# The backward weave of a gated attention pair: when ridden rows, sweep chunks and weights are loaded

## The chip, the cores and the metric

One core of one Trainium2 chip runs the whole kernel as one launch. The metric is device microseconds of one execution, median of several runs. The profile is of one further execution. Engines are named as the profile names them: PE (TensorE matmuls) with PEld (its weight loads), DVE (VectorE), ACT (ScalarE), POOL (GpSimd), SP (SyncE, which here only issues DMAs). Each of SP and POOL works through its own list in order, and an entry that waits holds all entries behind it.

## The reference

A token-wise gate mixes two attention branches over 2048 tokens of width 576, and all gradients are wanted.

```python
def _fwd_reference(A_x, A_wq, ..., B_Wo, B_seg_len, gate_w):
    ...
        scores = jnp.einsum('bhqd,bkd->bhqk', q, k) * Dh ** (-0.5)   # branch A: 32 query heads of 18, one key/value head
        p = _softmax(scores, axis=-1)
    ...
        for s in range(n_seg):                                       # branch B: 64 segments of 32 tokens
            xs = x[:, s * seg_len:(s + 1) * seg_len, :].copy()
            h = jnp.concatenate([mem, xs], axis=1)                   # 8 memory rows ahead of 32 tokens
            ...
            o = jnp.einsum('bhte,hed->btd', o, Wo)
            mem = o[:, :M, :].copy()                                 # the recurrence
    ...
    g = _sigmoid((x * gate_w).sum(-1, keepdims=True))
    return g * a + (1 - g) * b

def reference(...):
    _out, _vjp = jax.vjp(_f, A_x, A_wq, A_wk, A_wv, A_wo, B_mem0, B_Wq, B_Wk, B_Wv, B_Wo, gate_w)
    _grads = _vjp(grad_out)
    return (_out, *_grads)
```

Branch B's recurrence makes its backward pass a chain of 64 segments, one after the other, from segment 63 down to 0. Branch A's backward pass has no such chain.

## The kernel before

The stages follow each other: projections, a forward weave, a token stage (`b_bulk`, which does what of branch B's backward pass needs no chain), the backward weave, a stage behind the chain (`b_post`), the weight gradients and branch A's end. The change lies in the backward weave and in the last part of the token stage. Lines are those of the kernel before.

**The weave.** `weave` (L274) lays two generators into one program order: the chain `b_chain_bwd` (L1001) and the sweep `a_pass2` (L1910), with a third generator `bwd_weights` (L649) that loads weights. One step, number i, runs the sweep to its next `yield`, lets the chain go on if i is in `prime`, and then lets the weights go on by one load. First `lead` = 12 such steps run, in which the chain is let on only in steps 2 and 5 (its memsets and first loads). From then on every chain place is followed by a step, until the chain is at its end; what is left of the sweep would run last. The order is written out by hand (`manual_schedule`): no scheduler moves an instruction.

**The sweep** has 1024 pairs of heads and 128-query blocks, one per step. Step n issues `b_S` (scores, PE) of pair n+1 into a single PSUM buffer, `b_dP` (PE) of pair n, the exponential `b_E` (ACT, L1951) of pair n+1, two products `b_dS` (DVE, L1974) and four `b_acc` matmuls of pair n-1. Its input comes in chunks: chunk c holds the queries of pairs 4c to 4c+3 in one of three buffers `b_QS` of 256 KB. In the token stage, eight groups before its loop ends, `sweep_first` (L1903) loads chunks 0 and 1. Each later chunk is loaded by SP in steps n with n % 4 = 2 (`load`, L1926, issue at L1932): chunk n/4+2, which waits until the last `b_acc` of chunk c-3, two steps earlier, is done, and is first read by the `b_S` that is issued in step n+5.

**The chain.** A segment has 16 places, each ended by a `yield`; this text counts them 1 to 16. Segment 63 has no places 1 to 3. In places 1 to 3 the gradient of the 8 memory rows (`dm`) is projected with `WoT`. Place 4 builds `r_dOT`, `r_prod` and the first `mem_grad`; its POOL work ends with four small DMAs to `dOm_dram`. Place 5 takes the softmax back (`r_dS`, `r_dSB`). Places 6 to 15 hold 48 units of `heads`, which multiply `dT` with the weights `WT`: value weights first (to place 9), then query weights (to place 12), then key weights (to place 15). Place 16 turns the sum into the next `dm`. The tile `dT` has three parts of 32 columns per head: 8 columns come from `mem_cols` (L1168), in place 5 (value), 8 (query) and 9 (key), and 24 are token rows that ride along so that 32 columns are full. These ridden rows are loaded by `load_dT` (L1040, a DMA that transposes, issue at L1043) for the next segment: value in place 11, query in place 14, key in place 16. That is done for segments 54 to 0. `load_a`, `load_b` and `load_c` bring the other inputs of the next segment, in places 6, 9 and 12. `kv_mm` and `kv_out`, in segments 59 to 16, compute key and value gradients of tokens beside the chain, with loads on SP (L1076 to L1083) and stores on POOL.

**The weights.** `WT` has 24 tiles of 576 KB (value 0 to 7, query 8 to 15, key 16 to 23). The token stage loads 0 to 11, as its ring of buffers comes free. `bwd_weights` loads the rest, one per step, and then `WoT`:

```python
        for j in range(12, 24):
            self.load_WT(j, pool)
            yield
        for kt in range(4):
            self.nc.sync.dma_start(self.WoT[0][:, kt, :], self.st_WoT[kt])
            yield
        self.nc.sync.dma_start(self.WoT[1][:], self.st_WoTt[:])
        yield
```

So 17 loads stand in steps 0 to 16: twelve of 576 KB, four of 1 MB, one of 512 KB. `WoT` is first read in place 1 of segment 62.

**The loads' limit.** The DMAs of SP take turns on eight semaphores, and so do those of POOL: a DMA is not issued before the one eight entries ahead of it in the same list has landed.

Of the kernel before, what the change touches and what calls it, by code (L numbers as in the profile page):

```python
# [12 lines left out]
BF16 = mybir.dt.bfloat16  # L13
# [3 lines left out]
P = 128  # L17
# [29 lines left out]
class Kern:  # L47
# [229 lines left out]
    def weave(self, chain, sweep, lead, prime=(), early=()):  # L277
        steps = itertools.count()
        early = iter(early)

        def step():
            i = next(steps)
            next(sweep, None)
            if i in prime:
                next(chain)
            next(early, None)

        for _ in range(lead):
            step()
        for _ in chain:  # L290
            step()
        for _ in sweep:
            pass
# [708 lines left out]
    def b_chain_bwd(self, wot, sp, kd, kvp, keep, psum):  # L1002
        nc = self.nc
# [12 lines left out]
        f = lambda ap: ap.rearrange("p c q -> p (c q)")  # L1016
# [18 lines left out]
        def load_c(s):  # L1035
            nc.sync.dma_start(mrow["dx"][0:32].rearrange("p u e -> p (u e)"),
                              self.dmx_dram[s * 8:s * 8 + 8].rearrange("m (c u) w e -> (m c) (u w e)", u=8))
            nc.sync.dma_start(mrow["q"][:].rearrange("p u e -> p (u e)"), self.row_dram["q"][s])

        def load_dT(s, wi):  # L1040
            if 0 <= s < NSEG - KR:
                t0 = T - RIDE * (NSEG - KR - s)
                nc.sync.dma_start_transpose(dT[:, wi], self.xtok[("dq", "dk", "dv")[wi]][t0:t0 + 32, :])  # L1043
# [14 lines left out]
        def x_rows(s, x, src):  # L1058
            xq = sp.tile([P, 2, 32], BF16, name=f"r_xq{x}", bufs=1)
            nc.vector.transpose(f(xq[:]), src)  # L1060
            nc.gpsimd.dma_start(self.pq_dram[s // 4].rearrange("c i q s h x k -> (c i q) s h x k")
                                [:, s % 4, :, x, 32 * (s % 4):32 * (s % 4) + 32], xq[:])
# [65 lines left out]
        for s in reversed(range(NSEG)):  # L1128
# [12 lines left out]
            for k, parts in enumerate((((0, (0, 1, 2)),), ((0, (3, 4)), (1, (0, 1))), ((1, (2, 3, 4)),))):  # L1141
                if s == NSEG - 1:
                    break
                for j, kts in parts:
                    self.proj_part(pj[j], d_, self.WoT, j, kts)
                    if kts[-1] == 4:
                        self.evac(dOm[:, 4 * j:4 * j + 4, :].rearrange("p u e -> p (u e)"), pj[j][:], use="s")
                if k == 1:
                    x_rows(s, 0, pT[:, 0, :])
                yield  # L1150
            src = self.mem_T(dOm, psum, "r_x", 1)
            dOT = sp.tile([P, 8, 4, 8], BF16, name="r_dOT", bufs=1)
# [47 lines left out]
            def heads(n):  # L1200
                for _ in range(n):
                    wi, u, cp = next(units)
                    for g in range(4):
                        h, hf = 8 * (2 * cp + g // 2) + u, g % 2
                        self.mm(ph[32 * g:32 * g + 32, :], lhsT=dT[:, wi, h, :],
                                rhs=self.WTs(wi, h, 2 * GD * hf, 2 * GD),
                                start=(wi == 2 and u + cp == 0), stop=(wi == 1 and u + cp == 8), tp=(0, 32 * g))
# [26 lines left out]
            yield  # L1234
            kv_out(n0 + 1)
            heads(7)
            load_dT(s - 1, 2)
            if s:
                pad_in("p", nxt["pT"][:, 1, :])
            yield  # L1240
            heads(7)
            if s:
                load_c(s - 1)
            yield
# [4 lines left out]
            yield  # L1249
            kv_out(n0 + 2)  # L1250
            heads(7)
            load_dT(s - 1, 0)
            if n0 == -4:
                kv_load(0)
            yield
# [20 lines left out]
            dn = dm[1 - s % 2]  # L1276
            nc.scalar.copy(dn[:, :, 0:8], pm[:])
            nc.gpsimd.dma_start(self.dxr_dram[s], hs[0:64].rearrange("p k c -> p (k c)"))
            load_dT(s - 1, 1)
            yield  # L1280
        pt = psum.tile([P, 8, P], BF16, name="r_x", bufs=1)
        for kt in range(NKT):
# [618 lines left out]
        dq_.dma_start(self.qs_blk(b, 1).rearrange("a p c -> p a c"), qt[:].rearrange("p a t x -> p a (t x)"))  # L1901

    def sweep_first(self):  # L1903
        self.QS = [self.wr.tile([P, 2, 512], BF16, name=f"b_QS{c}", bufs=1) for c in range(2)]
        self.KVb = [self.wr.tile([P, 512], BF16, name="b_KV0", bufs=1)]
        self.nc.sync.dma_start(self.KVb[0][:], self.kv_dram[:, 0:512])
        for c in range(2):
            self.nc.sync.dma_start(self.QS[c][:], self.qs_dram[0, c])

    def a_pass2(self, keep, sp, kvp, psum):  # L1910
        nc = self.nc
        T, NTT = self.T, self.NTT
        KV = {}

        def load_KV(kb):
            if kb < 4:
                KV[kb] = self.KVb[kb % 2]
                if kb:
                    nc.sync.dma_start(KV[kb][:], self.kv_dram[:, kb * 512:kb * 512 + 512])

        self.QS.append(sp.tile([P, 2, 512], BF16, name="b_QS2", bufs=1))
        self.KVb.append(keep.tile([P, 512], BF16, name="b_KV1", bufs=1))
        load_KV(0)
        Q, S, E_, D_ = {}, {}, {}, {}
        NC = 4 * NPR * NTT // 4

        def load(c):
            if c < NC:
                p, q4 = (c // 4) % NPR, c % 4
                QS = self.QS[c % 3]  # L1930
                if c > 1:
                    nc.sync.dma_start(QS[:], self.qs_dram[p, q4])  # L1932
                Q[c] = (QS[:, 0, :], QS[:, 1, :].rearrange("p (a b) -> p a b", b=P))

        def pair(n):
            return n // (NPR * NTT), n // 4, n % 4

        def mm_u(dst, n, base):
            kb, c, j = pair(n)
            for i in range(2):  # L1940
                r = slice(base + 32 * i, base + 32 * i + 32)
                self.mm(dst[i], lhsT=Q[c][0][r, j * P:j * P + P], rhs=KV[kb][r, :],
                        tp=(base + 32 * i, 0))

        def mm_S(n):
            S[n] = psum.tile([P, 2, 512], F32, name="b_S", bufs=1)
            mm_u([S[n][:, i, :] for i in range(2)], n, 0)

        def ex(n):
            E_[n] = sp.tile([P, 2, 512], BF16, name="b_E", bufs=3)  # L1950
            nc.scalar.activation(E_[n][:], S.pop(n)[:], ACT.Exp, scale=SCALEA)  # L1951

        load(0)
        load(1)
        mm_S(0)
        ex(0)
        acc = None
        NS = NPR * NTT
        NP_ = 4 * NS
        for n in range(NP_ + 1):  # L1960
            if n < NP_:
                if n % 4 == 2:
                    load(n // 4 + 2)
                if n % NS == NS // 2:
                    load_KV(n // NS + 1)
                if n + 1 < NP_:
                    mm_S(n + 1)
                dP = [psum.tile([P, 512], F32, name="b_dP", bufs=3) for _ in range(2)]
                mm_u([t[:] for t in dP], n, 64)
                if n + 1 < NP_:  # L1970
                    ex(n + 1)
                D_[n] = sp.tile([P, 2, 512], BF16, name="b_dS", bufs=2)
                for i in range(2):
                    nc.vector.tensor_tensor(out=D_[n][:, i, :], in0=dP[i][:], in1=E_[n][:, i, :], op=ALU.mult)  # L1974
            if n > 0:
                o = n - 1
                if o % NS == 0:
                    acc = psum.tile([P, 512], F32, name="b_acc", bufs=1)
                SD = Q[o // 4][1]
                src = (D_.pop(o), E_.pop(o))  # L1980
                for i4 in range(4):
                    self.mm(acc[32 * i4:32 * i4 + 32, :], lhsT=SD[:, o % 4, 32 * i4:32 * i4 + 32],
                            rhs=src[i4 // 2][:, i4 % 2, :],
                            start=(o % NS == 0), stop=(o % NS == NS - 1), tp=(0, 32 * i4))
                if o % NS == NS - 1:
                    dkv = kvp.tile([P, 4, P], BF16, name="r_kvo", bufs=2)
                    nc.scalar.copy(dkv[:].rearrange("p i e -> p (i e)"), acc[:])
                    k0 = (o // NS) * 512
                    nc.gpsimd.dma_start(self.dkv_dram[:, k0:k0 + 512], dkv[:].rearrange("p i e -> p (i e)"))
            yield  # L1990
# [103 lines left out]
def build_full(tc, A_x, A_wq, A_wk, A_wv, A_wo, B_mem0, B_Wq, B_Wk, B_Wv, B_Wo, gate_w, grad_out, outs_raw,  # L2094
               dbg=None):
    nc = tc.nc
# [4 lines left out]
    k = Kern(tc, T, A_x, A_wq, A_wk, A_wv, A_wo, B_mem0, B_Wq, B_Wk, B_Wv, B_Wo, gate_w, grad_out, outs=outs)  # L2101
# [3 lines left out]
    with SB("const") as cpool, tc.tile_pool(name="dram", bufs=1, space=bass.MemoryType.DRAM) as dram:  # L2105
# [18 lines left out]
        with ExitStack() as man:  # L2124
# [39 lines left out]
            twp = tw.enter_context(SB("tw"))  # L2164
            with SB("a3s", RIGHT) as a3s, SB("a3k", RIGHT) as a3k, SB("rw") as rw, SB("rs") as rs, \
                    SB("rd") as rd, SB("rk") as rk, SB("rv") as rv, PS("rp") as rp, PS("a3p") as a3p:
                k.weave(k.b_chain_bwd(rw, rs, rd, rv, rk, rp), k.a_pass2(a3k, a3s, rv, a3p), 12, (2, 5),
                        k.bwd_weights(twp))
            wHs = ExitStack()
            wH = wHs.enter_context(SB("wH", RIGHT))  # L2170
# [84 lines left out]
```

## Time and profile before

| | us |
|---|---|
| median of 3 runs | 5364.2 (5357.48 to 5371.53) |
| the profiled execution | 5351.38 |
| its span, from first to last instruction | 5349.7 |
| backward weave, first `b_S` to the last `dm` (2670.55 to 4326.3) | 1655.8 |
| of it up to place 1 of segment 62 (2732.82) | 62.3 |

The page gives busy time of each engine, the span in 40 slices, DMA queues, the chain of work that ended last, and the costliest groups of instructions. Other views list instructions in order of time, the waits of one engine with what ended them, and busy time in chosen stretches. "idle before" in brackets is the time that the engine stood still ahead of an instruction, with what ended it. A matmul's duration is partly modelled, so the gaps say more than the busy shares.

### The profile page before, as it was taken

How to read it: one execution, taken by the hardware profiler on the slowest of the kernel's cores; microseconds unless marked ns; L12 is line 12 of the kernel's file. 1: busy time of each engine (PE TensorE's matmuls, PEld its weight loads, DVE VectorE, ACT ScalarE, POOL GpSimd, SP SyncE). 2: the span in 40 equal slices, each digit the busy share in tenths (PEclk: the TensorE clock that was granted, in tenths of full speed). 3: DMA queues.
4: the chain of work that ended last, by engine and by line, in shares of the span. 5: the costliest groups of instructions: out<-in, count | busy, mean ns of one | idle time of the engine just before them, and what ended most of it. 6: DMA issues, size and time to landing. Idle time of an engine off the chain costs nothing.

```text
span 5349.7 us, 218056 instructions
## 1 busy us (share of the span) xinstructions
PE 5023.2 (94%) x93298; PEld 2941.2 (55%) x93476; DVE 3619.4 (68%) x7146; ACT 3323.5 (62%) x4816; POOL 2421.1 (45%) x4634
## 2 busy tenths in 40 slices
PE   7999999999999998988879999999999999999999
PEld 5434555555555555777735555555554467764444
DVE  5337888888888887777778888888888831111112
ACT  4327888888888886666668888888887732111101
POOL 4004555555555554444436666666654321222223
PEclk9999999999999999999989999999999999999999
DMA  6655655665665445878866889888876679976653
GB/s 217 227 182 131 146 140 143 140 144 144 140 143 131 119 107 181 247 235 241 242 202 170 193 196 199 199 197 200 196 172 140 148 165 224 265 229 210 195 175 114
DMA packets 1115775, 961.45 MB, mean 180 GB/s; under 512 B 690738, under 2 KB 942139, under 8 KB 1105202
## 3 DMA queue, kind: packets, MB, share of 16 engines
q1 hardware_dynamic: 1013730, 702.18, 53.2%
q0 software_dynamic: 100928, 245.16, 15.2%
q8 instruction: 731, 11.98, 1.0%
q14 instruction: 242, 1.98, 0.1%
q10 hardware_dynamic: 144, 0.15, 0.0%
HBM read 521.16 MB, written 357.96 MB: 164 GB/s over the span
## 4 chain that ended last, share of the span: by engine, by line
PE 72%; ACT 9%; issue 9%; POOL 3%; DMA 2%; DVE 1%; SPq 1%; POOLq 0%; ACTq 0%; DVEq 0%
PE w_acc L82 12%; PE r_pj L82 7%; PE b_S L82 6%; PE a_S L82 6%; PE a_acc L82 5%; PE c_pj L82 5%; ACT b_E L1951 5%; PE b_acc L82 5%; PE r_x L82 5%; PE p_pb L82 4%; PE c_x L82 4%; ACT a_E L1778 4%; PE x_tr L87 3%; PE x_b L82 2%; PE x_po L82 2%
## 5 line engine op out<-in xcount | busy, mean ns | idle before, releaser
L1974 DVE TENSOR_TENSOR b_dS<-b_dP,b_E 128x512 bf16<-128x512 f32 x2048 | 1314.3, 683 | 224.7 <-issue 91.1
L1811 DVE TENSOR_TENSOR a_W<-a_dP,a_E 128x512 bf16<-128x512 f32 x2048 | 1313.0, 683 | 206.7 <-issue 76.8
L1951 ACT ACTIVATE b_E<-b_S 128x1024 bf16<-128x1024 f32 x1024 | 1048.8, 1024 | 285.4 <-PE b_dP L82 196.2
L1778 ACT ACTIVATE a_E<-a_S 128x1024 bf16<-128x1024 f32 x1024 | 1049.9, 1025 | 240.0 <-PE a_dP L82 192.7
L82 PEld LDWEIGHTS <-b_QS 32*128 32x128 bf16 (+1 forms) x8192 | 270.3, 92 | 522.8 <-issue 463.5
L82 PE MATMUL r_pj<-WT,r_dT 128*32 128x288 bf16 x12288 | 497.2, 287 | 6.0 <-issue 6.0
L82 PE MATMUL b_S<-b_KV,b_QS 32*128 32x512 bf16 x2048 | 405.1, 383 | 92.7 <-ACT b_E L1951 60.8
L82 PE MATMUL w_acc<-w_d,w_h 128*128 128x512 bf16 (+1 forms) x2352 | 470.9, 379 | 2.5
L82 PE MATMUL a_S<-a_QD,l_KV 32*128 32x512 bf16 x2048 | 399.6, 381 | 42.6 <-ACT a_E L1778 20.5
L82 PE MATMUL b_acc<-b_dS,b_QS 128*32 128x512 bf16 x2048 | 424.4, 393 | 0.2
L82 PE MATMUL a_acc<-a_E,l_VK 128*32 128x256 bf16 x8192 | 412.2, 278 | 5.0
L82 PE MATMUL b_acc<-b_E,b_QS 128*32 128x512 bf16 x2048 | 407.1, 394 | 0.0
L82 PE MATMUL b_dP<-b_KV,b_QS 32*128 32x512 bf16 x2048 | 403.8, 389 | 0.1
L82 PE MATMUL a_dP<-a_QD,l_KV 32*128 32x512 bf16 x2048 | 398.6, 385 | 0.1
L82 PEld LDWEIGHTS <-r_dT 128*32 128x32 bf16 x12288 | 336.4, 97 | 97.6 <-issue 10.6
L82 PEld LDWEIGHTS <-w_h 128*128 128x128 bf16 (+1 forms) x2688 | 230.0, 100 | 258.2 <-issue 6.6
L82 PEld LDWEIGHTS <-l_KV 32*128 32x128 bf16 x4096 | 150.1, 91 | 288.1 <-issue 264.4
L82 PE MATMUL a_acc<-a_W,l_WK 128*32 128x256 bf16 x4096 | 291.3, 273 | 0.4 <-DVE a_W L1811 0.3
L79 ACT CAST w_o<-w_acc 128x512 bf16<-128x512 f32 x54 | 31.6, 586 | 384.2 <-PE w_acc L82 358.7
L77 DVE CAST w_o<-w_acc 128x512 bf16<-128x512 f32 x54 | 37.4, 692 | 335.1 <-PE w_acc L82 307.2
L82 PEld LDWEIGHTS <-l_VK 128*32 128x32 bf16 x8192 | 128.9, 94 | 236.9 <-issue 233.1
L1092 POOL TENSOR_TENSOR r_kb<-r_ks,bmask 128x512 bf16<-128x512 bf16 x176 | 188.7, 1072 | 105.2 <-DMA r_ks<-px_dram 39.8
(482 smaller groups left out, 10609.6 us busy)
## 6 DMA issues: line engine op xcount, KB each, us to landing
b_QS<-qs_dram SPq DMA_DIRECT2D x256, 256.0 KB
dOx_dram<-p_tok SPq DMA_DIRECT2D x16, 1024.0 KB
c_vx<-vx_dram SPq DMA_DIRECT2D x64, 256.0 KB
krow_dram<-c_k POOLq DMA_DIRECT2D x64, 256.0 KB, 3.5
qrow_dram<-c_q POOLq DMA_DIRECT2D x64, 256.0 KB, 4.3
vrow_dram<-c_v POOLq DMA_DIRECT2D x64, 256.0 KB, 6.5
x_q<-qx_dram SPq DMA_DIRECT2D x32, 512.0 KB
x_k<-kx_dram SPq DMA_DIRECT2D x32, 512.0 KB
```

The costliest lines, as they stand in the source:

```text
L77: nc.vector.tensor_copy(out, in_)
L79: nc.scalar.copy(out, in_)
L82: return self.nc.tensor.matmul(out, lhsT, rhs, start=start, stop=stop, tile_position=tp, skip_group_check=True)
L87: return self.nc.tensor.transpose(out, in_, self.identB[b:b + nrows, b:b + nrows], tile_position=tp)
L1092: nc.gpsimd.tensor_tensor(out=B[:], in0=a[:].unsqueeze(2).to_broadcast([P, 4, 4, SEG]), in1=self.bmask[:, :, 0].unsqueeze(1).unsqueeze(3). ...
L1778: nc.scalar.activation(E_[n][:], S.pop(n)[:], ACT.Exp, scale=SCALEA)
L1811: nc.vector.tensor_tensor(out=W_[n][:, i, :], in0=dP[i][:], in1=E_[n][:, i, :], op=ALU.mult)
L1951: nc.scalar.activation(E_[n][:], S.pop(n)[:], ACT.Exp, scale=SCALEA)
L1974: nc.vector.tensor_tensor(out=D_[n][:, i, :], in0=dP[i][:], in1=E_[n][:, i, :], op=ALU.mult)
```

## The change

In `weave`, the weights go on in two of three steps. In the call, `lead` goes from 12 to 14. `sweep_first` loads three chunks instead of two, the third buffer moving from the sweep's own pool into the pool `wr`, which is opened ahead of the token stage. Chunks 3 to 9 are issued by GpSimd, all later ones by SP as before. The ridden rows are loaded in place 12 (value), in place 16 (query) and in place 2 of the segment that uses them (key). The title of the change counts places from the fourth one, so that these are its places 8, 12 and 14. What is computed stays the same.

```diff
@@ weave
-            next(early, None)
+            if i % 3:
+                next(early, None)
@@ b_chain_bwd, places 1 to 3
                 if k == 1:
                     x_rows(s, 0, pT[:, 0, :])
+                    load_dT(s, 1)
                 yield
@@ places 11 and 12
             heads(7)
-            load_dT(s - 1, 2)
             if s:
                 pad_in("p", nxt["pT"][:, 1, :])
             yield
             heads(7)
+            load_dT(s - 1, 2)
             if s:
                 load_c(s - 1)
@@ place 14
             heads(7)
-            load_dT(s - 1, 0)
@@ place 16
-            load_dT(s - 1, 1)
+            load_dT(s - 1, 0)
             yield
@@ sweep_first
-        self.QS = [self.wr.tile([P, 2, 512], BF16, name=f"b_QS{c}", bufs=1) for c in range(2)]
+        self.QS = [self.wr.tile([P, 2, 512], BF16, name=f"b_QS{c}", bufs=1) for c in range(3)]
...
-        for c in range(2):
+        for c in range(3):
             self.nc.sync.dma_start(self.QS[c][:], self.qs_dram[0, c])
@@ a_pass2
-        self.QS.append(sp.tile([P, 2, 512], BF16, name="b_QS2", bufs=1))
...
-                if c > 1:
-                    nc.sync.dma_start(QS[:], self.qs_dram[p, q4])
+                if c > 2:
+                    (nc.gpsimd if c < 10 else nc.sync).dma_start(QS[:], self.qs_dram[p, q4])
@@ build_full
-                k.weave(k.b_chain_bwd(rw, rs, rd, rv, rk, rp), k.a_pass2(a3k, a3s, rv, a3p), 12, (2, 5),
+                k.weave(k.b_chain_bwd(rw, rs, rd, rv, rk, rp), k.a_pass2(a3k, a3s, rv, a3p), 14, (2, 5),
```

## The prediction

> **What bounds the kernel now.** I began with the page: PE is busy for 94% of the span, but that is an average over stages. In its 40 slices PE drops to 8 in slices 20 and 21 only, and the granted clock to 8 in slice 20: the start of the backward weave (20 slices are 2674.9 us).
>
> ```profile
> span 5349.7 us, 218056 instructions
> ...
> PE   7999999999999998988879999999999999999999
> ...
> PEclk9999999999999999999989999999999999999999
> ```
>
> Next, busy time by stretch: last part of the token stage, start of the weave, its first full segments, its middle. Columns are length, then busy us (and instructions) of PE, PEld, DVE, ACT and POOL, granted clock, DMA share, GB/s.
>
> ```profile
> 2641.00:2671.00 30.00, 26.44 (x695) 20.61 (x684) 19.52 (x65) 18.62 (x41) 18.75 (x30) 1.00 0.77 248
> 2671.00:2736.00 65.00, 35.90 (x551) 14.48 (x554) 35.06 (x59) 29.67 (x34) 22.84 (x38) 0.66 0.96 300
> 2736.00:2836.00 100.00, 92.27 (x2016) 49.69 (x2012) 87.23 (x152) 77.77 (x100) 47.52 (x84) 1.00 0.52 129
> 3036.00:3536.00 500.00, 480.74 (x10260) 262.23 (x10248) 427.85 (x741) 411.37 (x549) 327.11 (x530) 0.99 0.90 197
> ```
>
> In the 65 us from 2671 PE works 35.9 us at a clock of 0.66, while the DMA engines are 0.96 busy: this stretch belongs to the DMAs. Later PE is 96% busy. The waits of PE, first in the start, then from 2736 to 4316, say what ends the rest:
>
> ```profile
> PE b_S L82 <- DMA b_QS<-qs_dram: 16.3, 4, 9.1
> PE r_x L82 <- POOL r_dOm L1137: 3.7, 1, 3.7
> ```
> ```profile
> PE b_S L82 <- ACT b_E L1951: 52.1, 191, 0.5
> PE b_S L82 <- DMA b_QS<-qs_dram: 7.2, 10, 2.0
> ```
>
> 16.3 us of the start are waits for sweep chunks. SP's list shows why they are late:
>
> ```profile
> 2672.11 0.92 SPq L1932 DMA_DIRECT2D b_QS<-qs_dram  x1
> 2682.18 0.60 SPq L1031 DMA_DIRECT2D r_kx<-kx_dram  x1
> 2691.08 0.34 SPq L1932 DMA_DIRECT2D b_QS<-qs_dram  x1
> ...
> 2714.62 0.32 SPq L656 DMA_DIRECT2D WoTt<-st_WoTt  x1
> 2715.47 0.59 SPq L1031 DMA_DIRECT2D r_kx<-kx_dram  x1
> ...
> 2716.68 0.45 SPq L1932 DMA_DIRECT2D b_QS<-qs_dram  x1
> ```
>
> Chunk 3 is issued at 2691.08, eight entries behind `r_kx`; the wait list of SP has 3.9 us there for `r_kx`. PE reads it at 2699.83, 8.7 us later, after 9.1 us of idling. Chunk 6, issued at 2716.68 right behind 2.5 MB of `WoT`, is read at 2730.10, 13.4 us later, after 5.99 us of idling.
>
> **Pace.** A step of the middle takes 1.55 us: `b_E` 1.02 and 0.53 until the next scores are there, one PSUM buffer. A segment of 16 steps has a floor of 24.8 us; the 62 from place 1 of segment 62 (2732.82) to that of segment 0 (4306.97) took 1574.2, so 36 us lie above the floor, of which 7.2 are waits for chunks.
>
> **The change, part by part.** All against the profiled span of 5349.7 us.
>
> *Third chunk in the token stage.* One load of 256 KB more in a stretch where DMA is 0.77 busy and PE 88%; SP's issue takes 0.34 to 0.92. Hidden behind PE: 0; with no cover +1 (256 KB at 248 GB/s). It takes the first wait (0.74 us at 2684.22) away, and 0.6 us of DMA (256 KB at some 410 GB/s) out of the start.
>
> *Chunks 3 to 9 by GpSimd.* Seven issues leave SP, where each also held weights behind its wait for `b_acc`, and seven of 0.55 to 0.84 us (POOL's own DMA rows) join POOL, busy for 22.8 of 65 us. The program gives each its place on POOL: 3 behind the memsets (end 2680.96), 4 alone, 5 behind the four DMAs of place 4, 6 behind the copy of place 8, 7 behind place 11, 8 behind place 16, 9 behind place 4 of segment 62. Behind chunk 5 queue the copy of `r_dT` and `r_dSB`, which PE wants only in place 8. Landing of a 256 KB load by POOL in this crowd is in no row. POOL's 16 and 64 KB DMAs there took 5.3 (`pq_dram`), 6.6 (`dmx_dram`) and 7.5 us (`dOm_dram`); SP's chunks 8.7 to 13.4 behind their own queue. I take 7.5, ends 5.3 and 13.4.
>
> The trace has POOL's small DMAs landing sooner than SP's chunks. The Trainium skill, page "DMA: Bandwidth & Descriptors", says two things. "Queues, rings and completion order": an engine goes round-robin between queues, which would let a POOL load pass SP's backlog. "Issuing engines are not separate DMA queues": issuing from another engine saves only issue time. By the first the 7.5 stands; by the second it would be 8.7 or more, which is rival B.
>
> *Walk through the start.* Steps 1 to 11 go on at 1.77 (rows 2687.76, 2689.53). Chunk 3 is issued at 2681 and lands at 2688.5, ahead of step 11 at 2691.3: the 9.1 us are gone. With lead 14 place 4 comes behind step 13 (2694.8) instead of 11. Its POOL wait of 3.7 us stays: step 14 at 2700.5, as step 12 followed 5.65 behind step 11. Chunk 5 goes out 2.8 us later, behind the DMAs of place 4, lands at 2710.8 and is wanted in step 19 at 2709.6: stall 1.2. Chunks 6 and 7 come out within 0.2 each. Place 1 of segment 62 is then due at some 2723.5 us.
>
> *Weights at two of three steps.* Ten instead of 14 weight loads stand ahead of `load_a` of segment 62, which waits for place 5. `WoT` falls behind `load_b`, which waits until PE is through place 8 (2709.3 in my walk). From there 6.1 MB must come (four `WoT` 4.2, `WoTt` 0.5, `load_b`, `load_c` 0.9, chunks 0.5): at 410 GB/s (5 us stretches from 2696 to 2711 moved 399 to 413) 14.9 us, 2724, plus some 2 us for landing and up to 2.5 for the transposing load in `load_a` (the rate falls to 238 and 227 GB/s in 2681 to 2691, behind such a load): 2726 to 2729. So `WoT`, not the chunks, ends the start; place 3 goes at 2728.5 where it now goes at 2737.25: **-8.5 us**. Ends: -12 if `WoT` never waits, and 0 if all 19.5 MB end as late as now (DMA falls off at 2731).
>
> *Lead 14.* Two steps move from the end of the weave to its start; places 7 and 8 of segment 0 then run alone. Now they take two steps, 3.1 us; alone 1.03 for 28 `heads` matmuls and about 1 for 12 and a `mem_grad`: **-1**.
>
> *Ridden rows.* Per segment three transposing loads move on SP (issue 1.3 us each). With lead 14 chunk loads stand in places 4, 8, 12, 16 instead of 2, 6, 10, 14, and each of them now has one transposing load ahead. Today chunk load 6 stands right behind `load_a`, which waits for place 5 and takes about 3.4 us to issue, and is wanted five steps (7.75 us) later; load 14 stands behind the query rows, which wait for the value rows' landing, eight entries ahead (27.3 us in 28 waits of SP). After the change the first has 3.1 us more, and the second pair is apart. The waits of 7.2 us should nearly go; the last key rows get 7 steps, 10.9 us, before `mem_cols` writes, against 14 now. Their landing is in no row; the nearest bound is that the query rows' load, three places (4.65 us) behind the value rows', waits up to 2.2 us for their landing: some 7 us. I take **-7**; ends -12 (each wait's after-effect too) and +27 (rival C).
>
> Sum: -8.5 - 1 - 7 = **-16.5 us**. Span 5333; against the median of the runs shown, which lies 12.8 above the profiled execution, 5364.2 - 16.5 = **5348 us**.
>
> **Rivals.**
> *B, bytes set the start.* For: DMA busy 0.96, 300 GB/s, and the same bytes are due before place 3. Against: place 3 waits for `WoT` alone, and `load_a`, `load_b` and chunks after it were part of those bytes. Chunks then take 8.7 to 13.4 by POOL, place 8 and with it `WoT` slip by 5 to 6: start -3, rest -8 cut to -4: about -7, 5357.
> *C, the value rows' load in place 12 makes every chunk late.* It stands with `load_b`, `r_ks`, `r_kr` and `load_c` ahead of the chunk load of place 12, all behind the wait for place 8: 4.2 to 5.9 us of issue. The chunk is wanted 9 steps (13.9 us) after place 8. If it lands more than 8 us after issue, PE waits. At 0.5 us in each of 55 segments: +27 -9.5 = +18, 5382. Against: today's budget is 7.75 us from the chunk load's own step, and of some 250 chunk loads in the middle ten made PE wait.
> *D, it does not do what it says.* The waits move one for one (chunk wait to `WoT` wait, place 6 to place 12): 5364.
>
> **Chances.** Forecast 0.50, B 0.26, D 0.12, C 0.12. Range: forecast 5339 to 5358 by its own ends (-25 with the best of each part; -6 with `WoT` 3 us before its worst and no gain in the middle); taking in B, D and part of the scatter of the runs (5357 to 5371), 5334 to 5368, which leaves C out and little below. No change can be told from a measurement within about 0.3% (16 us). The forecast sits on that line: 0.45 faster (nearly all of its 0.50, less some of its lower half, more of B's lower end), 0.41 within, 0.14 slower (C, and some of D).
>
> **What would show it.** Right: no idling of `b_S` on `b_QS` above 2 us before 2720; place 1 of segment 62 (`r_pj<-WoT`) near 2724 with a wait for `WoT` of a few us after it; chunk waits from there to the sweep's end under 2 us; the weave's segments at 25.3 instead of 25.4. Wrong: `b_S` idle on `b_QS` with POOL as issuer; `r_dT` (ACT) waiting for a DMA; `WoT` landing behind 2732; chunk waits above 10 us in the middle. A change outside 2671 to 4330 would be none of my reasons.

## The result, and the profile after

| | before | after |
|---|---|---|
| median of 20 runs each, us | 5365.4 (5343.39 to 5380.35) | 5352.51 (5336.19 to 5362.64) |
| ratio, 95% interval | | 0.9978 [0.9969, 0.9988] |
| span of the profiled execution, us | 5349.7 | 5344.9 |

By the ratio the changed kernel is about 12 us faster (the medians differ by 12.9). The interval leaves 1 out, although single runs of either kernel spread over more than that (37 us before, 26 after). The median lies 4.5 us above the forecast of 5348. Timed once more, together with other kernels, it came out at 0.9992 [0.9978, 1.0005], an interval that does not leave 1 out.

The page of after, the lines that answer to the first fence of the prediction:

```profile
span 5344.9 us, 218260 instructions
...
PE   7999999999999998888979999999999999999999
...
PEclk9999999999999999999989999999999999999999
```

The clock's line is that of before, and PE's differs only in two slices of the token stage (16 and 19, counted from 0): a change of 0.2% is not to be seen in 40 slices. The stretches tell more. In this profile the sweep begins 8.65 us later than in the one of before (first `b_E` at 2679.81, there 2671.16), because the token stage ahead of it, which the change leaves almost alone, took longer in this execution. So the stretches are taken 9 us later; columns as in the prediction.

```profile
2650.00:2680.00 30.00, 25.53 (x667) 19.80 (x665) 18.65 (x63) 18.36 (x40) 19.12 (x31) 1.00 0.78 248
2680.00:2745.00 65.00, 40.84 (x587) 15.73 (x590) 38.32 (x65) 32.26 (x37) 26.53 (x44) 0.68 0.95 296
2745.00:2845.00 100.00, 92.74 (x2008) 49.44 (x2000) 86.82 (x151) 77.22 (x99) 47.71 (x84) 0.99 0.50 130
3045.00:3545.00 500.00, 485.43 (x10413) 266.81 (x10405) 432.62 (x749) 416.02 (x555) 332.57 (x537) 1.00 0.89 199
```

In the start PE gets more done (40.8 us against 35.9), but the last two numbers are nearly those of before: DMA engines 0.95 busy, 296 GB/s against 300. The waits of PE in the start (total, times, longest):

```profile
PE r_pj L82 <- DMA WoT<-st_WoT: 7.8, 4, 3.6
PE r_x L82 <- POOL r_dOm L1138: 3.7, 1, 3.7
PE b_S L82 <- DMA b_QS<-qs_dram: 1.6, 2, 1.3
PE r_pj L82 <- DMA WoTt<-st_WoTt: 0.6, 1, 0.6
```

The waits for chunks fell from 16.3 to 1.6 us, and 8.4 us of waits for `WoT` and `WoTt` came in, of which before had none. They lie in place 1 to 3 of segment 62, as PE's timeline shows (start, duration, instruction, idle before it):

```profile
2731.78 0.40 PE L82 MATMUL r_pj<-WoT,dm 128*32 128x512 bf16 x4 [0.96 <-DMA WoT<-st_WoT]
2734.63 0.62 PE L82 MATMUL r_pj<-WoT,dm 128*32 128x512 bf16 x4 [2.46 <-DMA WoT<-st_WoT]
2738.87 0.62 PE L82 MATMUL r_pj<-WoT,dm 128*32 128x512 bf16 x4 [3.62 <-DMA WoT<-st_WoT]
2741.35 0.62 PE L82 MATMUL r_pj<-WoT,dm 128*32 128x512 bf16 x4 [0.78 <-DMA WoT<-st_WoT]
2742.60 0.62 PE L82 MATMUL r_pj<-WoTt,dm 128*32 128x512 bf16 x4 [0.63 <-DMA WoTt<-st_WoTt]
```

Why so late is in SP's list and in what it moved:

```profile
2717.62 1.78 SPq L655 DMA_DIRECT2D WoT<-st_WoT  x2
...
2721.49 2.84 SPq L655 DMA_DIRECT2D WoT<-st_WoT  x2
2727.76 0.32 SPq L657 DMA_DIRECT2D WoTt<-st_WoTt  x1
```

By their semaphores the five loads landed 14 to 17 us after issue, the last near 2742.6. Two stretches of after, the first that of these landings, the second the whole start up to place 3 (last number: GB/s):

```profile
2718.00:2743.00 25.00, 13.99 (x227) 6.08 (x231) 12.49 (x22) 10.00 (x12) 5.42 (x10) 0.82 0.90 311
...
2679.80:2745.80 66.00, 41.64 (x591) 15.99 (x594) 39.12 (x66) 33.18 (x38) 26.73 (x45) 0.68 0.94 292
```

In the middle, from 2746 to 4316, the waits of 7.2 us for chunks are nearly gone:

```profile
PE b_S L82 <- ACT b_E L1951: 53.3, 198, 0.5
...
PE b_S L82 <- DMA b_QS<-qs_dram: 0.9, 1, 0.9
```

To compare executions that begin the weave at different times, all that follows counts from the first `b_E` of the sweep. "Place 1" and "place 3" are the first `r_pj` that reads `WoT` and the first `r_x` that reads `WoTt` in segment 62; "middle" runs from the 9th copy of `dm` to the last but one, "last segment" from there to the last, "weave" from the first `b_E` to the last `dm`. "Chunks" and "WoT" are PE's waits for them. All in us, worked out from each trace:

| profile | place 1 | place 3 | in the start: chunks / WoT | middle | chunks in it | last segment | weave |
|---|---|---|---|---|---|---|---|
| before | 61.7 | 66.5 | 16.3 / 0 | 1371.4 | 7.0 | 19.8 | 1654.9 |
| before_again | 61.7 | 65.9 | 15.9 / 0 | 1368.8 | 4.3 | 19.8 | 1650.5 |
| after | 52.0 | 66.0 | 1.6 / 8.4 | 1365.5 | 0.9 | 18.4 | 1646.5 |
| after_again | 51.5 | 65.7 | 0.7 / 7.7 | 1371.2 | 1.4 | 18.4 | 1651.8 |
| rows_back | 51.7 | 65.2 | 1.8 / 7.1 | 1366.2 | 3.1 | 18.4 | 1646.8 |
| chunks_sp | 55.7 | 67.5 | 6.0 / 5.2 | 1364.0 | 1.6 | 18.4 | 1646.0 |
| chunks_sp_again | 53.7 | 67.4 | 4.8 / 7.3 | 1367.2 | 3.3 | 18.4 | 1648.4 |
| weights_each | 59.0 | 63.6 | 1.7 / 0 | 1367.3 | 4.0 | 18.4 | 1645.7 |
| lead12 | 51.8 | 64.1 | 0.7 / 5.4 | 1379.3 | 11.4 | 19.8 | 1660.7 |
| before_lead14 | 60.3 | 63.8 | 9.8 / 0 | 1367.3 | 4.9 | 18.4 | 1645.1 |
| before_lead14_again | 60.0 | 63.4 | 10.6 / 0 | 1363.1 | 4.7 | 18.4 | 1640.6 |
| before_lead16 | 63.1 | 66.5 | 9.8 / 0 | 1365.2 | 4.4 | 20.2 | 1649.7 |
| lead22 | 65.4 | 68.8 | 1.5 / 0 | 1369.0 | 0.6 | 15.8 | 1650.3 |
| more_bytes | 55.2 | 74.8 | 2.7 / 14.8 | 1373.2 | 3.7 | 18.4 | 1662.9 |

One profile is not enough for the middle: two of the same kernel lie 2.5 to 5.7 us apart. Place 3 and the last segment repeat within 0.6 us.

### The profile page after: what moved, and what is told of

It reads as the page before. It is cut to its first block, busy times and chain, and to the rows that moved or that the text cites. A ratio compares the mean times of both kernels' runs of the same rounds, so it can differ in the third digit from the quotient of the medians.

```text
span 5344.9 us, 218260 instructions
## 1 busy us (share of the span) xinstructions
PE 5037.9 (94%) x93476; PEld 2943.8 (55%) x93476; DVE 3620.1 (68%) x7146; ACT 3322.5 (62%) x4816; POOL 2423.1 (45%) x4641
## 4 chain that ended last, share of the span: by engine, by line
PE 74%; ACT 9%; issue 7%; POOL 3%; DMA 2%; SPq 1%; DVE 1%; POOLq 0%; ACTq 0%; DVEq 0%
PE w_acc L82 12%; PE r_pj L82 7%; PE b_S L82 6%; PE a_S L82 6%; PE a_acc L82 5%; PE c_pj L82 5%; ACT b_E L1951 5%; PE b_acc L82 5%; PE r_x L82 5%; PE p_pb L82 4%; PE c_x L82 4%; ACT a_E L1779 4%; PE x_tr L87 3%; PE x_b L82 2%; PE x_po L82 2%
## 5 line engine op out<-in xcount | busy, mean ns | idle before, releaser
L82 PE MATMUL b_S<-b_KV,b_QS 32*128 32x512 bf16 x2048 | 404.9, 383 | 75.0 <-ACT b_E L1951 63.8
```

The source lines that it names most:

```text
L82: return self.nc.tensor.matmul(out, lhsT, rhs, start=start, stop=stop, tile_position=tp, skip_group_check=True)
```

## The experiments

The times of the runs that were timed in rounds, against the kernel before on the same chip in the same rounds (11 or 12 executions each, 17 to 35 of before):

| kernel | median, us | before, us | ratio, 95% interval |
|---|---|---|---|
| rows_back | 5339.97 | 5348.18 | 0.999 [0.9979, 1.0001] |
| chunks_sp | 5351.55 | 5348.18 | 1.0012 [1.0, 1.0023] |
| weights_each | 5341.01 | 5348.18 | 0.9983 [0.9971, 0.9996] |
| before_lead14 | 5336.57 | 5346.9 | 0.9977 [0.9963, 0.9991] |
| lead22 | 5345.18 | 5346.9 | 1.0 [0.9987, 1.0013] |
| lead12 | 5349.05 | 5349.58 | 1.0003 [0.9991, 1.0015] |
| before_lead16 | 5350.11 | 5349.58 | 1.0 [0.9987, 1.0014] |
| after_again | 5346.15 | 5349.58 | 0.9992 [0.9978, 1.0005] |
| chunks_sp_again | 5346.79 | 5349.58 | 0.9992 [0.9983, 1.0002] |
| before_lead14_again | 5335.32 | 5345.79 | 0.9987 [0.9974, 1.0] |

My theory after the result: bytes set the start, and the gain is what two further sweep steps cost nothing there. Its rivals: the moved rows, GpSimd's queue or the slower weights carry it.

### The kernel before once more

> The kernel before once more, unchanged, to learn how far single stages differ between two executions. The backward weave (first b_S exponential to last dm copy) took 1654.9 us; if stage lengths repeat, it is within 2 us of that, place 3 of segment 62 (first product with the tail of WoT into r_x) again lies 66 us behind the weave's start, and the stretch from segment 55 to the last dm is again 1391 us. If they don't repeat, no comparison of single profiles below 5 us holds. The token stage ahead of the weave, which differed by 6 us between the two profiles, is expected to scatter by several us.

Its sweep began at 2684.74, 13.6 us later than in the first profile of the same kernel, and its weave took 1650.5 against 1654.9, 4.4 us apart where 2 were expected; place 3 came at 65.9, as expected. So the start of the sweep, and with it a span, scatters by more than the whole gain, and one profile against another tells nothing of the sum.

### The parts undone one by one

The rows back in their old places:

```diff
@@ places 1 to 3
                     x_rows(s, 0, pT[:, 0, :])
-                    load_dT(s, 1)
@@ place 11
+            load_dT(s - 1, 2)
@@ place 12
-            load_dT(s - 1, 2)
@@ place 14
+            load_dT(s - 1, 0)
@@ place 16
-            load_dT(s - 1, 0)
+            load_dT(s - 1, 1)
```

> The changed kernel with the ridden rows loaded in places 11, 14 and 16 as before (lead 14, three chunks, GpSimd and two of three steps kept). Theory: the moved rows took away the waits for chunks in the middle; then the stretch from segment 55 to the last dm goes back from 1383.9 to about 1389, waits of b_S for b_QS there return to 5 to 10 us, and the ratio to the kernel before goes from 0.998 to 0.999. Rival: lead 14 alone moved the chunk loads away from load_a and that was enough: 1384, no more than 2 us of such waits, ratio 0.998.

The waits for chunks in the middle came back in part, 3.1 us against 0.9 and 1.4, but the middle took 1366.2 us, between the two of after. The ratio of 0.999 is the one expected, the waits of 5 to 10 us are not. Moving the rows is worth some 2 us of waits here, too little to see in the time.

All chunks issued by SP:

```diff
-                    (nc.gpsimd if c < 10 else nc.sync).dma_start(QS[:], self.qs_dram[p, q4])
+                    nc.sync.dma_start(QS[:], self.qs_dram[p, q4])
```

> The changed kernel with chunks 3 to 9 issued by SP again. Theory: bytes set the start, so waits for chunks come back (10 us or more) and waits for WoT shrink by as much; place 3 of segment 62 stays 66 us (within 1.5) behind the weave's start, ratio 0.998. Rival: GpSimd's chunks are worth something by themselves: place 3 at 70 or later, ratio above 0.999.

Chunk 3 landed 25.4 us after the first `b_E` instead of 13.3, and PE waited 6.0 us for it; in exchange the waits for `WoT` fell from 8.4 to 5.2, and place 3 came 1.5 us later. The theory had asked for 10 us of chunk waits and a ratio of 0.998. The ratio of 1.0012 did not fit a weave as short as after's, so I ran it again:

> The changed kernel with all chunks issued by SP once more. Its stages were those of the changed kernel (weave 1646.0 us) but its ratio 1.0012 [1.0, 1.0023]. Theory 'the queue of the chunks decides nothing, and that ratio was an unlucky set of executions': the ratio is that of the changed kernel of this call within 0.15 per cent, the weave 1645 to 1648 us. Rival 'chunks on SP's queue cost what the profiles do not show': the ratio is again 1.0 or more, and 0.2 per cent or more over the changed kernel.

Now it was level with the changed kernel of the same rounds (5346.79 and 5346.15), with place 3 at 67.4 us as in its first profile (67.5). GpSimd's queue brings the chunks early and buys some 1.5 us at place 3, which the times cannot show. That the first ratio was chance is likely, not shown: the stages do not hold a cause for it.

Weights in every step again:

```diff
-            if i % 3:
-                next(early, None)
+            next(early, None)
```

> The changed kernel with a weight load in every step again. Theory: bytes set the start: WoT is asked for earlier, but place 3 of segment 62 stays within 1.5 us of 66 behind the weave's start, waits for WoT shrink and waits for chunks grow. Rival: in the changed kernel WoT is late because its loads stand behind SP's waits for places 5 and 8 and behind the eight outstanding loads; then place 3 comes at 62 or earlier and the ratio falls to 0.997.

Neither came out: the waits for `WoT` are gone and those for chunks did not grow, place 3 comes 2.4 us earlier than in after (the theory allowed 1.5, the rival asked for 62 or earlier), and the ratio is 0.9983. `WoT` had landed by 49.7 us and `WoTt` by 54.7, 8.9 us ahead of place 3, so here their landing does not set it. The waits of PE in its start:

```profile
PE b_dP L82 <- DVE b_dS L1973: 4.8, 1, 4.8
PE r_x L82 <- POOL r_dOm L1137: 3.7, 1, 3.7
PE b_S L82 <- DMA b_QS<-qs_dram: 1.7, 2, 1.3
```

The new 4.8 us come from `load_a` of segment 62: its `r_pT` is issued only 46.7 us after the first `b_E` (at 2709.15), and a transpose on DVE that needs what is made of it (`r_pq`, idle 5.4 us before it) stands ahead of a `b_dS`. On SP the transposing load just ahead of `r_pT` takes 11.7 us to issue, against 1.5 to 3.7 in before and after, while the four loads of `WoT` are landing; no row names what held it. With chunks early and weights early, the rows are what is late. Thinning the weights to two of three steps shows no gain: 0.9983 without it.

### Are bytes the limit of the start?

The changed kernel with the first two of `WoT`'s four loads issued twice, 2.1 MB more of the same data:

```diff
-            self.nc.sync.dma_start(self.WoT[0][:, kt, :], self.st_WoT[kt])
+            for _ in range(2 if kt < 2 else 1):
+                self.nc.sync.dma_start(self.WoT[0][:, kt, :], self.st_WoT[kt])
```

> The changed kernel with the first two of WoT's loads issued twice each, 2 further loads of 1 MB in all if a slice is 512 KB (the profile's issue list tells), with the same data. Theory 'bytes set the start': place 3 of segment 62 comes later by the time that the further bytes take at the 299 GB/s of this stretch, about 3.5 us for each MB, and all of it shows as waits of r_pj and r_x for WoT and WoTt. Rival 'the order of landings or the sweep sets the start': the further loads hide behind the sweep's steps and place 3 stays within 1 us of 66.0.

Place 3 moved from 66.0 to 74.8 us, 8.8 us for 2.1 MB, where 2.1 MB at 299 GB/s asks for 7.0. Its waits in the start:

```profile
PE r_pj L82 <- DMA WoT<-st_WoT: 14.1, 4, 8.7
...
PE b_S L82 <- DMA b_QS<-qs_dram: 2.7, 1, 2.7
```

That looks like the theory, but the edit adds more than bytes. A repeated load writes the part of the tile that the first one is still filling, and SP stood still for that landing. Its waits in the same stretch:

```profile
SPq L656 <- DMA WoT<-st_WoT: 19.7, 2, 12.1
```

In after SP never waits for `WoT` there. From the first issue of `WoT` to place 3 (37.1 us) the DMA engines were only 0.68 to 0.85 busy here, in after 1.04 and then 0.82 up to the last landing. So the 8.8 us hold waiting as well as bytes, and the run does not tell them apart.

What the traces do show is narrower. In after the start ends with the landing of `WoT`: `WoTt` lands at 62.8 us, place 3 follows at 66.0, and the DMA engines were fully busy (1.03) for the first 50 us. In before the same five loads had landed by 54.9 us, 11.6 us ahead of place 3, and in those 11.6 us the DMA engines were 0.43 busy: there PE waits for no `WoT`, and its last long wait is for chunk 6, which lands at 58.9. The mean rates over the whole start are close (19.26 MB in 66.0 us in after, 292 GB/s; 19.52 MB in 66.5 us in before, 294), but a mean that takes in such an idle end is no limit. That bytes set the start of every kernel is not shown.

### The lead alone, and without the lead

The kernel before with a lead of 14 and nothing else:

```diff
-k.weave(k.b_chain_bwd(rw, rs, rd, rv, rk, rp), k.a_pass2(a3k, a3s, rv, a3p), 12, (2, 5),
+k.weave(k.b_chain_bwd(rw, rs, rd, rv, rk, rp), k.a_pass2(a3k, a3s, rv, a3p), 14, (2, 5),
```

> The kernel before with one edit: 14 sweep steps ahead of the chain instead of 12; ridden rows, chunks and weights as before. Theory 'the lead alone': the middle (9th dm copy to last) falls from 1390 us in the two profiles of the kernel before to 1384 to 1386, the waits of b_S for chunks in the middle from 4.5 to 7.2 us to 3.1 or less, as in rows_back, and the weave (first b_E to last dm) from 1652.7 to about 1647: the time about 0.1 per cent under the kernel before. Rival 'the moved rows, the third chunk or POOL's queue are needed': the middle stays at 1388 to 1391, the two lone steps only lengthen the start's waits, and the time is that of the kernel before within 0.05 per cent.

One number of the diff gave 0.9977, as much as the whole change and twice what was expected of it; the waits for chunks in the middle, 4.9 us, did not fall to 3.1. Its waits in the start:

```profile
PE b_S L82 <- DMA b_QS<-qs_dram: 9.8, 2, 9.2
PE r_x L82 <- POOL r_dOm L1137: 3.7, 1, 3.7
```

The long wait for chunk 3 stays, the one of 6 us for chunk 6 has gone: with two more steps ahead of place 4, chunk 5 is issued 32.0 us after the first `b_E` (before: 41.3) and `WoT`'s loads from 29.1 to 34.7 (before: the last two at 41.8 and 42.3, next to chunks 5 and 6). The same bytes flow with fewer gaps, 19.51 MB in 63.7 us, 306 GB/s, with the DMA engines 0.97 instead of 0.93 busy; place 3 comes 2 to 3 us earlier although two more steps have run by then. Once more:

> The kernel before with a lead of 14 alone, once more, since the changed kernel's own ratio came out as 0.9978 and then as 0.9992. Theory 'the lead alone carries the gain, about 0.1 to 0.2 per cent': place 3 at 63 to 65 us after the first b_E (63.76 in its first profile), last segment 18.4 us, waits for chunks in the middle 3 to 6 us, the weave 1645 to 1649 us, the ratio 0.9975 to 0.9992. Rival 'its 0.9977 was a lucky set of executions and it is the kernel before': place 3 at 66 us or later or the middle over 1370 us, and a ratio of 0.9995 or more.

0.9987 [0.9974, 1.0], weave 1640.6, start and last segment as in its first run to 0.4 us. The theory's numbers hold but for the weave, for which 1645 to 1649 was said; its middle is the shortest of all fourteen profiles.

The other way round, the changed kernel with a lead of 12:

```diff
-a3p), 14, (2, 5),
+a3p), 12, (2, 5),
```

> The changed kernel with 12 sweep steps ahead of the chain, all else as changed (moved rows, third chunk, POOL's queue, weights at two of three steps). Theory 'the lead carries the gain': the last segment takes 19.8 us again, place 3 comes at 65 to 67 us, the middle keeps what fewer chunk waits give it (9th to last but one dm copy 1365 to 1368 us, at most 3 less than the 1370.1 of the two profiles of the kernel before): the weave takes 1648 to 1652 us, the time is 0 to 0.09 per cent under the kernel before. Rival 'the other parts carry it': the weave takes 1647 or less and the ratio is that of the changed kernel, 0.998.

1.0003: without the lead the other parts together show no gain. That much the theory had said; the rest it had wrong. Place 3 came at 64.1 (65 to 67 was said), the weave took 1660.7, and the middle took 1379.3 us, with more waiting for chunks than in before. Waits of PE in the middle, and in the second fence of SP from 3036 to 3536:

```profile
PE b_S L82 <- DMA b_QS<-qs_dram: 11.4, 13, 1.7
```
```profile
SPq L1932 <- DMA r_dT<-dvx_dram: 23.8, 17, 3.3
```

L1932 is the chunk's load. It now stands behind the moved rows' landing, 23.8 us in 500; in the same 500 us of before and of after L1932 never waits for them. PE pays on the first step of three of the four chunks of a segment (steps 4, 8 and 12 of 16: 3.9, 3.8 and 3.7 us in all). So the moved rows go with the lead of 14, which carries the chunk loads two places on. The waits are not the whole of the long middle, though: in this profile the granted clock also stood at 0.5 for 20.5 us of it, longer than in any other (0 to 13.7), and one profile does not part the two.

Against lead12 the changed kernel also shows what two more steps do in the new layout: place 3 comes 1.6 to 1.9 us later (64.1 to 66.0 and 65.7), and the last segment gives 1.4 back. At the two ends the lead gains nothing there; what it gains lies in the middle, 8 to 14 us by single profiles. In the old layout it is the other way round: place 3 and the last segment come 2 to 3 and 1.4 us earlier, with no sure change in the middle.

### More lead

> The kernel before with 16 sweep steps ahead of the chain: chunk loads stand at the same places of a segment as with 12, since a chunk serves four steps. Theory 'the lone steps at the end become cheaper ones beside the chain': the last segment takes 17.0 us (1.4 less for each two steps: 19.8, 18.4, 17.0), place 3 comes at 63 to 66 us, the middle is that of lead 14 or of lead 12, the weave takes 1643 to 1649 us. Rival 'lead 14 gains by the place of its chunk loads': the middle's waits for chunks are back at 4.5 to 7.2 us, the middle at 1369 to 1371, and the time between the kernel before and lead 14.

The theory that each further step is free fell here, and the rival did not come out either. The waits for chunks in the middle are 4.4 us, within what leads of 12 and 14 show in the old layout (4.3 to 7.0), so no effect of the chunk loads' place is seen there. But place 3 is back at 66.5, and the last segment takes 20.2 us instead of the 17.0 expected, although only three steps of the sweep are left in it. Behind them PE waits for POOL, which it does not do there with a lead of 12 or 14:

```profile
PE r_x L82 <- POOL r_dSB L261: 1.6, 1, 1.6
```

That is half of the 3.2 us; the other half was not followed.

> The changed kernel with 22 sweep steps ahead of the chain instead of 14. Theory 'the start is bound by bytes': place 3 of segment 62 stays at 66 us (to 68) after the first b_E, since the eight further lone steps fit into waits for WoT (8.4 us) and into the time in which the chain has little to do; the last segment's lone steps fall by eight, each worth the difference between a step of the sweep alone and one among the chain's (0.6 us by the last segment's fall of 1.4 us for two steps): 2 to 5 us less than the changed kernel. Rival 'the start is bound by the sweep's own work and chunks': eight further steps of about 2 us ask for four further chunks before the weights, place 3 comes at 75 us or later, waits for chunks return in the start (over 5 us), and the time is 4 us or more above the changed kernel.

Neither was right: place 3 came at 68.8 us, 0.8 outside the theory's range and far from the rival's 75, chunks are waited for 1.5 us only, and the ratio of 1.0 shows no gain. `WoT` is not waited for at all. ACT's timeline has the lone steps 1.77 us apart against 1.55 later, and the granted clock was 0.50 in the stretch in which they lie (third number from the end) and 1.00 from 2720 on:

```profile
2693.40 1.02 ACT L1951 ACTIVATE b_E<-b_S 128x1024 bf16<-128x1024 f32 x1 [0.75 <-PE b_dP L82]
2695.17 1.02 ACT L1951 ACTIVATE b_E<-b_S 128x1024 bf16<-128x1024 f32 x1 [0.74 <-PE b_dP L82]
```
```profile
2671.00:2718.00 47.00, 30.65 (x313) 9.52 (x316) 32.13 (x53) 25.58 (x27) 18.03 (x29) 0.50 1.03 345
```

The last segment is 15.8 us, the chain with no step beside it, and the 2.6 us gained there are given back at place 3 (66.0 to 68.8). Of the leads that ran, 12 and 14 in both layouts, 16 in the old and 22 in the new, only 14 has a timing whose interval leaves 1 out: three of its eight do; the other leads were timed once each.

### The changed kernel once more

> The changed kernel once more, on the chip and in the rounds of the others of this call. Its weave again takes 1646 to 1647 us (1646.5 in its first profile), with the 9th to last but one dm copy at 1365 to 1367 us; the ratio again 0.997 to 0.999. If the first middle of 1365.5 us was chance, it comes at 1368 or more.

The ratio is at the upper end of the range said, its weave (1651.8) and its middle are outside: 1371.2 us with waits for chunks of 1.4 us, so by its own test the first middle of 1365.5 was chance. Two stretches, the middle of after_again and of before_lead14_again (first busy time: PE):

```profile
2937.30:4308.50 1371.20, 1302.90 (x27978) 710.34 (x27978) 1185.60 (x2053) 1109.20 (x1456) 808.88 (x1343) 1.00 0.82 184
```
```profile
2927.90:4290.90 1363.00, 1299.33 (x27978) 708.75 (x27975) 1184.77 (x2052) 1109.64 (x1456) 808.97 (x1342) 1.00 0.83 185
```

The same 27978 matmuls took PE 1302.9 and 1299.3 us; over all fourteen profiles it is 1297 to 1306 (with 27964 matmuls in lead22's). This scatter is as large as what was sought in the middle. It goes with the granted clock, which here and there in the middle falls to 0.5 for 3.4 or 6.8 us: not once in chunks_sp and before_lead16 (PE busy 1297.4 and 1298.0 us), for 10.2 us in all in after_again and for 20.5 us in lead12 (1305.9).

## Why the prediction was right, and where its steps were not

- *The start, -8.5 us by place 3: mis-sized.* Place 3 came 66.0 and 65.7 us after the first `b_E`, in before 66.5 and 65.9: a gain of 0.3. The walk held up to `WoT`: its first load was due at 38.1 us and went out at 37.8, place 1 was due at 2723.5, which is 52.3 us after the first `b_E`, and came at 52.0 and 51.5, and chunks 4 to 8 landed 6.3 to 10.0 us after issue (chunk 3 3.5) where 7.5 was assumed. What failed is the next step, "at 410 GB/s (5 us stretches from 2696 to 2711 moved 399 to 413) 14.9 us". From there to the last landing it took 25 us, for two reasons. That stretch moved 311 GB/s, since a peak of 15 us had been taken for a rate; and it moved 7.9 MB, not the 6.1 that the sum lists. I had set the end of 0 at "all 19.5 MB end as late as now", and that is near what happened (`WoTt` landed at 62.8 us; in before the DMA engines fell off at 60). The waits went from chunks to `WoT`, as rival D said of the start. Rival B was right that little would be left of the gain in the start, but not by its own steps: chunks did not take 8.7 to 13.4 us, and `WoT` was not issued later.
- *B's rule.* The Trainium skill, page "DMA: Bandwidth & Descriptors", section "Issuing engines are not separate DMA queues", says that loads run on the same 16 DMA engines whoever issues them, so that another issuer saves issue time alone. For the end of the start the traces agree nearly: 66.0 and 65.7 us by GpSimd, 67.5 and 67.4 by SP. For chunk 3 they do not: by GpSimd it landed 12 us sooner, of which earlier issue is 4.4 us (9.7 against 14.1) and a shorter landing 7.8 (3.5 against 11.3). That it passed the loads that SP had queued is the likely reason, not one that a run shows.
- *Lead 14, -1: the last segment gave -1.4 (19.8 to 18.4).* But this term is the one on which the gain hangs, and I counted only its end. In before_lead14 the two steps more that stand ahead of place 3 cost less than nothing: place 3 comes 2 to 3 us earlier. Alone it gave 0.9977 and 0.9987, and no kernel with a lead of 12, 16 or 22 gained (1.0003, 1.0, 1.0). Start and last segment explain some 4 us of it; the rest lies in middles that scatter by as much.
- *Ridden rows, -7: too large.* Waits for chunks in the middle fell from 7.0 and 4.3 us to 0.9 and 1.4, some 4.5 us; 7.2 was the longer of two executions. Of these the moved rows give about 2 (rows_back, before_lead14: 3.1 to 4.9). The middle itself gained 1.8 us in the mean of two profiles (1370.1 to 1368.3), within its scatter. Rival C's mechanism, a chunk load behind the rows' landing, did not show with lead 14 and did with lead 12 (SP's 23.8 us).
- *Third chunk, 0:* its own share was not tried alone. With chunks 3 to 9 by GpSimd it took away 16.3 us of waits that the bytes gave back.
- *The sum, -16.5:* right in sign and, in the first timing, near in size (-12; in the second about -4), by terms that were not: that the number came near is luck. The start gave almost nothing, the middle less than said, the lead more. Of the first -12 us the weave of one profile explains 6 (1652.7, the mean of two of before, to 1646.5), that of the second 1. The rest is not settled: the stages outside the weave scatter by more.
- *"It does not do what it says"* (rival D) had the form of the start right, wait for wait, and of the whole probably wrong, by the two timings of before_lead14. The rows, the queue and the weights could each be undone without a loss that two timings agree on.
- *A reading of the page:* the prediction says that PE drops to 8 in slices 20 and 21 only. Its line has 8 in slices 15 and 17 to 19 and 7 in slice 20, counted from 0. The table of stretches, on which the argument rests, is read rightly.

What stays open: by what mechanism the lead of 14 gains, in the old layout (why place 3 comes earlier with 14 than with 12 or 16) and in the new one (the middle); what the start's end would be if bytes alone set it; and whether the changed kernel is at all different from the kernel before with a lead of 14 (0.9978 and 0.9992 against 0.9977 and 0.9987: not told apart).

## What to carry to other kernels

Before a wait is taken away in a stretch where the DMA engines are 0.95 busy, list all bytes that must still land and divide them by a mean rate, not by the best 15 us: the wait may only move to another load, as here from the chunks to `WoT`. Two steps of work that waits for nothing cost nothing there in the old layout (place 3 from 66.5 and 65.9 to 63.8 and 63.4), but four brought it back to 66.5, and in the new layout two cost some 1.7 us: such a number is to be tried, not argued. When a change has four parts, run each alone: here a single number gave as much as the whole, and one of the other parts seems to need it not to lose. An edit that is to add bytes must add nothing else: a load repeated into the same tile also adds a wait.

## What was not expected of the hardware

- 256 KB loads by GpSimd's queue landed 2.8 to 11.4 us after issue in the starts of the six kernels that issue them so (DMA engines 0.88 to 0.98 busy), by SP's 2.7 to 12.0 us (chunks_sp): the same spread. What the other queue changed was which chunk fell to which end of it (chunk 3: 3.5 to 8.9 against 10.9 and 11.3), and issue up to 7 us sooner (chunk 7: 41.0 against 48.2 us after the first `b_E`).
- The mean DMA rate of the start stays within 285 to 307 GB/s in all fourteen profiles, whatever the order of the loads, while 5 us stretches of it in after range from 228 to 413 with the engines 0.90 to 1.07 busy: busy engines do not mean the same bytes.
- PE's busy time for the same 27978 matmuls of the middle varies from 1297 to 1306 us at a mean granted clock of 1.00 to 0.99, and the start of the weave from 2662 to 2685 us after the span's start.
